# A fused adaLN, linear-attention and SwiGLU block: the order of the first query tiles, their PSUM banks and VectorE's list

## The chip, the cores and the metric

The kernel runs on one core of one Trainium2 chip. The metric is the device time of one execution in microseconds (us). Times of a kernel are medians over several executions; the profile is of one further execution. Below, PE is the matrix engine TensorE, PEld its weight loads, DVE is VectorE, ACT is ScalarE, POOL is GpSimd, and SP is the engine whose queue issues nearly all DMAs.

## The reference

One transformer block with x of 2048 rows and 1024 columns (bf16), a conditioning vector c, and a hidden width of 3584. Cut to what matters:

```python
sa, ca, ga, sb, cb, gb = split(silu(c) @ w_mod)          # six vectors of 1024
h = layernorm(x) * (1 + ca) + sa
q, k, v = heads(h @ wqkv)                                # 32 heads of 32
phi = lambda t: where(t > 0, t + 1, exp(t)) + 1e-6
pq, pk = phi(q), phi(k)
kv, z = einsum('bhsd,bhse->bhde', pk, v), einsum('bhsd->bhd', pk)
o = (pq @ kv) / (pq @ z + 1e-6)
x = x + ga * (o @ wo)
h = layernorm(x) * (1 + cb) + sb
x = x + gb * ((silu(h @ w_gate) * (h @ w_up)) @ w_down)
```

## The kernel before

The 2048 rows are 16 tiles of 128 rows, in four chunks of 512 rows. The columns of q and of k are eight tiles (`nt`) of 128 each, and the 1024 input columns are eight steps (`dt`) of a product. A q or k tile of one chunk is thus eight matmuls of 128 x 128 by 512 that accumulate in one PSUM bank. There are eight banks (0 to 7).

Instructions are recorded one after the other into a list for each engine (`_Prog`), and each engine runs its list strictly in order. Waits are derived from the recorded order: an instruction waits for the last conflicting access to its SBUF bytes, and for the last access of another engine to its PSUM bank. So the order in which the Python code records operations is the order of each engine's work, and an engine that waits holds back all that was recorded behind. All instructions appear in the profile with one line, that of the recorder (L176), so the tile names tell them apart.

The part that is changed runs in about the first 80 us. `HT[0]` and `HT[1]` hold the normalised, transposed and modulated input of the even and the odd chunks. Chunk 0 comes first, in `q_phase_chunk0`, while the weights are still being loaded: seven q tiles are kept open at the same time in the banks `qb = [1, 2, 3, 4, 6, 7, 5]`, and advance together step by step as weights and modulated input arrive (`q_part`). Bank 0 meanwhile takes the small products that give the modulation vectors (`mod_sc`: matmuls of one column) and the bias that stands in for the shift of `dt` 0 to 5 (`bias_mm`, read out by `bias_fin` into `BIASQ`). The second half of the `WSA` weights, which the last shift product needs, is among the late loads. `fin_sa` casts the product on DVE, and `bias_mm` needs its result. The eighth q tile is computed at the end, in bank 0, after `bias_fin` has emptied it. `h0_shift` then adds the shift to the four steps that did without it, for the k tiles.

`q_phi` evacuates each q tile on ACT (exp and relu with the bias), into four slots of `E1`/`RL` and four of `E1X`/`RLX`; `q_min` and `q_add` finish it on DVE. Between these, DVE prepares chunk 1: statistics of row tiles 5 to 7 (tile 4's are made on ACT by `act_stats`), reciprocal roots on POOL, `ln1_xn` (normalise), a transposing DMA on SP's queue for each row tile (`th_dma`), and `th_mod(1, ...)`, the modulation of `HT[1]`, in halves of 256 columns (row tiles 4 and 5, then 6 and 7).

After that come the k groups: `k_group(0, 0..7)` for chunk 0, then for each further chunk eight k groups and eight q groups. A group takes the next bank of `next_bank`. `phi_evac` evacuates it on ACT (exp into one of the four slots of `E1`, in turn) and DVE finishes two groups at a time (`phi_flush`). Between the groups, dictionaries (`kside` for chunk 0, `s1` to `s3` for chunks 1 to 3) hold side work by the number of the group it follows: statistics, normalisation, transposes and `th_mod` of the chunk after. `th_mod(2, dt)`, which prepares chunk 2's `HT[0]`, runs on ACT for odd `dt` and on DVE for even, after the q groups 9 to 11 of chunk 1. From there on the kernel goes through the linear attention and the feed-forward part, which the change does not touch.

The groups are counted by `next_bank` from 0 (chunk 0's first k group): 8 to 15 are chunk 1's k groups, 16 to 23 its q groups, 24 to 31 chunk 2's k groups.

Of the kernel before, what the change touches and what calls it, by code (L numbers as in the profile page):

```python
# [5 lines left out]
FP32 = mybir.dt.float32  # L6
# [3 lines left out]
ALU = mybir.AluOpType  # L10
# [252 lines left out]
def bass_adaLN_cond__linear_attn_block__swiglu_ffn__prompt_kernel(  # L263
# [22 lines left out]
    with ExitStack() as es:  # L286
# [6 lines left out]
        def T(name, off, shape, dt):  # L293
            n = 1
            for s_ in shape[1:]:
                n *= s_
            assert off % 32 == 0 and off + n * mybir.dt.size(dt) <= ARENA, (name, off, shape)
            return nc.alloc_sbuf_tensor_at(name, shape, dt, offset=base + off)
# [47 lines left out]
        RL = T("rl", 188 * KB, [128, 4, 512], BF16)  # L346
        E1X = T("e1x", 192 * KB, [128, 4, 512], BF16)
        RLX = T("rlx", 196 * KB, [128, 4, 512], BF16)
        ACC = T("acc", 192 * KB, [128, D], FP32)
        MHL = T("mhl", 196 * KB, [128, 2, D], BF16)  # L350
        MHLT = T("mhlt", 192 * KB, [128, 2 * NDT, 128], BF16)
# [131 lines left out]
        def ln1_xn(st, c0=0, c1=D):  # L483
            P.dve("tensor_scalar", out=XRES[:, st, c0:c1], in0=XRES[:, st, c0:c1],
                  scalar1=MV[:, st, 0:1], scalar2=RSTD[:, st:st + 1], op0=ALU.subtract, op1=ALU.mult)
# [7 lines left out]
        def th_dma(st):  # L493
            buf, j = (st // 4) % 2, st % 4
            xbar(HT[:, buf, :, j * 128:(j + 1) * 128], XRES[:, st, :])
# [12 lines left out]
        def mod_sc(w, c0, ms, kts=range(NDT)):  # L508
            for m in ms:
                for kt in kts:  # L510
                    P.pe("matmul", out=PS[:, 0, c0 + m:c0 + m + 1], lhsT=w[:, kt, m * 128:(m + 1) * 128],
                         rhs=SILUC[:, kt:kt + 1], start=mod_first[0], stop=(kt == NDT - 1), skip_group_check=True)
                    mod_first[0] = False
# [5 lines left out]
        def fin_sa(m, n, cast=False):  # L519
            if cast:  # L520
                P.dve("tensor_copy", out=MODTMP[:, m:m + n], in_=PS[:, 0, m:m + n])
            P.dve("tensor_copy", out=MODCOL[:, 1, m:m + n], in_=PS[:, 0, m:m + n])
# [5 lines left out]
        def h0_shift(dt):  # L528
            P.dve("tensor_scalar", out=HT[:, 0, dt, :], in0=HT[:, 0, dt, :], scalar1=MODCOL[:, 1, dt:dt + 1],
                  scalar2=None, op0=ALU.add)  # L530
# [47 lines left out]
        def act_stats(st, passes=(0, 1)):  # L578
            junk0 = HT[:, 1, 0:2, :] if st < 4 else JUNK1[:]
            for i in passes:  # L580
                fn_, sc_, acc_ = ((ACT.Identity, 1.0 / D, SUMX), (ACT.Square, D ** -0.5, SUMSQ))[i]
                P.act("activation", out=junk0, in_=XRES[:, st, :].rearrange("p (a b) -> p a b", a=2),
                      func=fn_, scale=sc_, accum_out=acc_[:, st:st + 1])
# [15 lines left out]
        def act_var(st):  # L599
            P.dve("scalar_tensor_tensor", out=MV[:, st, 1:2], in0=SUMX[:, st:st + 1], scalar=SUMX[:, st:st + 1],  # L600
                  in1=SUMSQ[:, st:st + 1], op0=ALU.mult, op1=ALU.subtract)
            P.dve("tensor_scalar", out=VE[:, st:st + 1], in0=MV[:, st, 1:2], scalar1=-1.0, scalar2=EPS, op0=ALU.mult,
                  op1=ALU.add)
# [8 lines left out]
        def ln1_xn_sum(st, c0=0, c1=D):  # L612
            P.dve("tensor_scalar", out=XRES[:, st, c0:c1], in0=XRES[:, st, c0:c1],
                  scalar1=SUMX[:, st:st + 1], scalar2=RSTD[:, st:st + 1], op0=ALU.subtract, op1=ALU.mult)

        def pool_pow(st):
            P.pool("tensor_tensor", out=RSTD[:, st:st + 1], in0=VE[:, st:st + 1], in1=NEGHALF[:, 0:1], op=ALU.pow)
# [78 lines left out]
        def q_part(nt, bank, dts):  # L696
            for dt in dts:
                P.pe("matmul", out=PS[:, bank, :], lhsT=WQK[:, dt, nt * 128:(nt + 1) * 128],
                     rhs=HT[:, 0, dt, :], start=(dt == 0), stop=(dt == 7))
# [3 lines left out]
        def next_bank():  # L703
            i = qk_ctr[0]
            qk_ctr[0] += 1
            return (1, 2, 3, 4, 6, 7, 5, 0)[i % 8] if i < 40 else i % 5 + 1

        def q_group(ch, nt):
            buf, bank = ch % 2, next_bank()
# [39 lines left out]
        def mod_row_b(bank, i, dst):  # L749
# [3 lines left out]
            P.wait_for("sp", [wr])  # L753
            P.dma("mdr%d" % i, dst[:], MDR[i].unsqueeze(0).to_broadcast([128, D]))

        def q_slot(nt):
            return (E1, RL) if nt < 4 else (E1X, RLX)

        def q_phi(nt, bank):
            for buf, fn_ in zip(q_slot(nt), (ACT.Exp, ACT.Relu)):  # L760
                P.act("activation", out=buf[:, nt % 4, :], in_=PS[:, bank, :], func=fn_, bias=BIASQ[:, nt:nt + 1])

        def q_min(nts):
            for nt in nts:
                e = q_slot(nt)[0][:, nt % 4, :]
                P.dve("tensor_scalar", out=e, in0=e, scalar1=1.0, scalar2=1e-6, op0=ALU.min, op1=ALU.add)

        def q_add(nts):
            for nt in nts:
                e, r = q_slot(nt)  # L770
                P.dve("tensor_tensor", out=PQT[:, nt, 0:512], in0=r[:, nt % 4, :], in1=e[:, nt % 4, :], op=ALU.add)

        def q_phase_chunk0():
            qb = [1, 2, 3, 4, 6, 7, 5]
            fin_ca(2, 2)
            for dt in (2, 3):
                h0_first(dt, "dve")
            for nts, dts in ((range(3), (0,)), (range(3), (1,)), ((3, 4, 5, 6), (0, 1))):
                for nt in nts:
                    q_part(nt, qb[nt], dts)  # L780
            for nt in range(7):
                if nt == 4:
                    mod_sc(WCA, 8, range(4, 8))
                    fin_ca(4, 4)
                    for dt in (4, 5):
                        h0_scale_only(dt)
                q_part(nt, qb[nt], (2, 3))
            act_stats(4, (0,))
            for nt in range(7):
                if nt == 6:  # L790
                    mod_sc(WSA, 0, range(6, 8))
                    fin_sa(6, 2)
                    for dt in (6, 7):
                        h0_scale(dt)
                q_part(nt, qb[nt], (4, 5))
            mod_sc(WSA, 0, range(4, 6))
            fin_sa(4, 2, True)
            for dt in (4, 5):
                h0_shift(dt)
            for nt in range(7):  # L800
                if nt == 2:
                    bias_mm((4, 5))
                q_part(nt, qb[nt], (6,))
            for nt in range(7):
                if nt == 1:
                    mod_sc(WSA, 0, range(4), range(4))
                if nt == 3:
                    mod_sc(WSA, 0, range(4), range(4, 8))
                    fin_sa(0, 4, True)
                    ln_ops[1][0]()  # L810
                if nt == 5:
                    bias_mm(range(4))
                    bias_fin()
                q_part(nt, qb[nt], (7,))
            ln_ops[1][1]()
            ln_ops[1][2]()
            ln1_rstd1(5)
            for i, dt in enumerate((4, 5, 0, 1, 2, 3, 6, 7)):
                P.pe("matmul", out=PS[:, 0, :], lhsT=WQK[:, dt, 896:1024], rhs=HT[:, 0, dt, :], start=(i == 0),
                     stop=(i == 7))  # L820
            for dt in range(4):
                h0_shift(dt)
            ln1_xn(5)
            th_dma(5)
            for nt in range(2):
                q_phi(nt, qb[nt])
            act_stats(4, (1,))
            for nt in range(2, 8):
                q_phi(nt, qb[nt] if nt < 7 else 0)
            for f in ln_ops[2]:  # L830
                f()
            act_var(4)
            pool_pow(4)
            for f in ln_ops[3]:
                f()
            ln1_rstd2(6)
            ln1_xn_sum(4)
            th_dma(4)
            q_min((0, 1))
            for st in (6, 7):  # L840
                ln1_xn(st)
                th_dma(st)
            q_add((0, 1))
            for nts in ((2, 3), (4, 5)):
                q_min(nts)
                q_add(nts)
            qk_ctr[0] = 0

        def add(d, k, f):
            d.setdefault(k, []).append(f)  # L850
# [1 line left out]
        kside = {}  # L852
        ln_ops = [ln1_stats_ops(4 + jj) for jj in range(4)]

        for c0 in (0, 256):
            for dt in range(NDT):
                add(kside, 1, lambda dt=dt, c0=c0: th_mod(1, dt, c0, c0 + 256))
        add(kside, 1, lambda: q_min((6, 7)))
        add(kside, 1, lambda: q_add((6, 7)))
        for jj, k in ((0, 3), (1, 4)):  # L860
            add(kside, k, lambda jj=jj: act_stats(10 + jj))
        q_phase_chunk0()
        for st in range(12, 16):
# [384 lines left out]
```

## Time and profile before

| | us |
|---|---|
| median of 3 executions | 828.32 |
| lowest and highest | 827.97, 828.67 |
| the profiled execution, device time | 827.71 |
| its span, first to last instruction | 826.0 |
| PE busy | 816.3 (99%) |
| DVE busy | 312.2 (38%) |
| ACT busy | 197.0 (24%) |
| POOL busy | 41.0 (5%) |

By stretches of the span (us busy of each engine, the granted PE clock is 1.00 in all):

| stretch | what runs | PE | DVE | ACT |
|---|---|---|---|---|
| 12.0 to 21.2 | q tiles of chunk 0, first steps | 9.12 of 9.20 | 2.33 | 2.02 |
| 21.2 to 29.3 | last steps, shift, bias, eighth q tile | 7.85 of 8.10 | 4.50 | 2.86 |
| 29.3 to 43.1 | k groups of chunk 0 | 13.69 of 13.80 | 13.10 | 13.77 |
| 43.1 to 56.9 | k groups of chunk 1 | 13.75 of 13.80 | 13.55 | 6.99 |
| 56.9 to 70.7 | q groups of chunk 1 | 13.75 of 13.80 | 11.98 | 10.97 |

How to read it: durations of neighbouring instructions overlap at their ends, so sums can come to a little more or less than the time passed. Matmul ends are modelled, and a few matmul records are missing; the distance from one matmul's start to the next is the more exact measure. A row of the timeline gives start, length, engine, line, operation, output and inputs, count, and in brackets how long the engine was idle before it and what released it.

### The profile page before, as it was taken

Reading aid. Unit: us, or ns where it says so; the run is one execution under the profiler, and the core shown is the slowest. Engines: PE = TensorE matmul, PEld = TensorE weight load, DVE = VectorE, ACT = ScalarE, POOL = GpSimd, SP = SyncE. Lnnn points to the kernel's source line nnn. Section 1 sums busy time; section 2 is a strip of 40 time slices with the busy share of each in tenths; the row PEclk is TensorE's granted clock in tenths of the full one; section 3 lists DMA queues with packets and bytes.
Section 4 is the critical chain, followed back from the end, with each engine's and each line's share of the span. In section 5 each row is a group of like instructions: output and inputs, shape, how many; then the busy total and the mean of one; then the engine's idle time right before and its main releaser. Section 6 shows DMA issues by size and latency. Waiting matters only on the chain.

```text
span 826.0 us, 10436 instructions
## 1 busy us (share of the span) xinstructions
PE 816.3 (99%) x4243; PEld 375.9 (46%) x4322; DVE 312.2 (38%) x672; ACT 197.0 (24%) x338; POOL 41.0 (5%) x58
## 2 busy tenths in 40 slices
PE   8999999999999999999999999999999999999998
PEld 4544444444444444444444444444444444444444
DVE  5798988477945521111221112122111111221111
ACT  4758642123341111011111101111110111111011
POOL 1110000000130000020000003000000300000000
DMA  9969756865698995600455570045557004553000
GB/s 316 297 139 223 167 159 149 181 175 211 149 253 245 296 249 153 166 26 26 136 151 151 153 174 25 23 131 153 151 152 182 27 19 126 151 152 88 0 26 26
DMA packets 199392, 119.32 MB, mean 144 GB/s; under 512 B 58024, under 2 KB 183088, under 8 KB 199344
## 3 DMA queue, kind: packets, MB, share of 16 engines
q1 hardware_dynamic: 199328, 118.65, 53.8%
q8 instruction: 34, 0.56, 0.3%
q14 instruction: 14, 0.11, 0.0%
q10 hardware_dynamic: 16, 0.00, 0.0%
HBM read 100.67 MB, written 4.33 MB: 127 GB/s over the span
## 4 chain that ended last, share of the span: by engine, by line
PE 98%; issue 1%; DMA 0%; DVE 0%; POOL 0%; SPq 0%
PE ps L176 98%; DMA xres<-in_A_x_dram 0%; POOL rstd L176 0%; DVE xres L176 0%; DVE stats L176 0%; SPq L176 0%; DVE ht L176 0%; DVE ve L176 0%; DVE mv L176 0%; DVE modcol L176 0%
## 5 line engine op out<-in xcount | busy, mean ns | idle before, releaser
L176 PE MATMUL ps<-h2t,gug 128*128 128x512 bf16 x878 | 210.1, 379 | 0.9
L176 PE MATMUL ps<-h2t,guu 128*128 128x512 bf16 x878 | 209.9, 379 | 0.9
L176 DVE TENSOR_TENSOR at<-sg,ps 128x512 bf16<-128x512 bf16 x112 | 77.0, 687 | 282.8 <-PE ps L176 270.6
L176 ACT ACTIVATE sg<-ps 128x512 bf16<-128x512 f32 x112 | 66.9, 597 | 309.7 <-PE ps L176 298.3
L176 PEld LDWEIGHTS ps<-h2t,guu 128*128 128x128 bf16 x896 | 87.7, 98 | 105.7
L176 PEld LDWEIGHTS ps<-h2t,gug 128*128 128x128 bf16 x896 | 87.6, 98 | 105.5
L176 PE MATMUL ps<-wd_a,at 128*128 128x512 bf16 (+1 forms) x502 | 111.9, 377 | 0.5
L176 PE MATMUL ps<-ht,wqk 128*128 128x512 bf16 x499 | 110.7, 379 | 0.9 <-DVE ht L176 0.2
L176 PE MATMUL ps<-wd_b,at 128*128 128x512 bf16 (+1 forms) x377 | 84.6, 377 | 0.4
L176 PEld LDWEIGHTS ps<-wd_a,at 128*128 128x128 bf16 x512 | 50.1, 98 | 59.6
L176 DVE TENSOR_TENSOR ut<-att,gb_b 128x512 bf16<-128x512 bf16 (+1 forms) x32 | 13.6, 426 | 167.5 <-ACT att L176 167.5
L176 PEld LDWEIGHTS ps<-ht,wqk 128*128 128x128 bf16 x512 | 49.2, 98 | 58.9 <-DVE ht L176 1.0
L176 ACT ACTIVATE att<-ps 128x512 bf16<-128x512 f32 (+1 forms) x32 | 17.4, 591 | 182.1 <-PE ps L176 182.1
L176 PEld LDWEIGHTS ps<-wd_b,at 128*128 128x128 bf16 x384 | 37.6, 98 | 44.7
L176 PE MATMUL ps<-pk,xres 128*128 128x512 bf16 x250 | 55.4, 379 | 0.6 <-issue 0.5
L176 PE MATMUL ps<-mw,pqt 128*128 128x512 bf16 x249 | 55.4, 379 | 0.5 <-issue 0.2
L176 POOL TENSOR_SCALAR h2t<-h2t,modcol 128x512 bf16<-128x512 bf16 x32 | 26.5, 846 | 383.0 <-DMA h2t<-xn 383.0
L176 ACT ACTIVATE e<-ps 128x512 bf16<-128x512 f32 x56 | 33.3, 611 | 31.8 <-PE ps L176 15.8
L176 ACT ACTIVATE junk<-xres 128x1024 bf16<-128x1024 bf16 x26 | 27.6, 1063 | 45.9 <-DVE xres L176 34.2
L176 PEld LDWEIGHTS ps<-mw,pqt 128*128 128x128 bf16 x256 | 24.8, 98 | 30.0 <-issue 0.5
L176 PEld LDWEIGHTS ps<-pk,xres 128*128 128x128 bf16 x256 | 24.6, 98 | 30.1 <-issue 1.3
L176 DVE SCALAR_TENSOR_TENSOR xres<-ps,xres 128x512 bf16<-128x512 f32 x32 | 21.5, 688 | 11.6 <-PE ps L176 11.3
(111 smaller groups left out, 337.8 us busy)
## 6 DMA issues: line engine op xcount, KB each, us to landing
gug<-in_B_w_gate_dram SPq DMA_DIRECT2D x56, 512.0 KB, 4.0
guu<-in_B_w_up_dram SPq DMA_DIRECT2D x56, 512.0 KB, 5.3
xres<-in_A_x_dram SPq DMA_DIRECT2D x20, 256.0 KB, 4.4
rb<-recip_den SPq DMA_DIRECT2D x8, 512.0 KB, 11.7
stgx<-in_w_mod_dram SPq DMA_DIRECT2D x2, 2048.0 KB, 9.3
wd_a<-in_B_w_down_dram SPq DMA_DIRECT2D x4, 1024.0 KB, 7.7
out_dram<-xres SPq DMA_DIRECT2D x31, 128.0 KB, 1.7
xres<-in_A_x_dram SPq DMA_DIRECT2D x3, 1024.0 KB, 6.5
```

Source lines behind the costliest of these rows:

```text
L176: return getattr(e, method)(**kw)
```

## The change

Four things are changed together. The dt=7 step of all seven open q tiles is done before the last shift products instead of between them, so tile 0 ends first; ACT copies it from its bank to a new SBUF tile `QRAW` (fp32), and the eighth q tile accumulates in tile 0's bank, its matmuls laid around the last shift products and the bias product. The q tiles are evacuated in the order `QORD` = 1 to 7, then 0 (from `QRAW`), and take their slots in that order. The bank rotation of `next_bank` starts with bank 0 and differs for the groups 24 to 39. DVE's list is put in another order: tile 4's variance and normalisation come earlier, its transpose goes out before tile 5's, the first half of `th_mod(1, ...)` moves from the side work into the end of `q_phase_chunk0`, the last four q tiles are finished after the fourth k group, and `act_stats(10)` and `act_stats(11)` on ACT follow one group later.

```diff
--- before.py
+++ after.py
@@ -346,6 +346,7 @@
         RL = T("rl", 188 * KB, [128, 4, 512], BF16)
         E1X = T("e1x", 192 * KB, [128, 4, 512], BF16)
         RLX = T("rlx", 196 * KB, [128, 4, 512], BF16)
+        QRAW = T("qraw", 202 * KB, [128, 512], FP32)
         ACC = T("acc", 192 * KB, [128, D], FP32)
         MHL = T("mhl", 196 * KB, [128, 2, D], BF16)
         MHLT = T("mhlt", 192 * KB, [128, 2 * NDT, 128], BF16)
@@ -703,7 +704,11 @@
         def next_bank():
             i = qk_ctr[0]
             qk_ctr[0] += 1
-            return (1, 2, 3, 4, 6, 7, 5, 0)[i % 8] if i < 40 else i % 5 + 1
+            if i < 24:
+                return (0, 2, 3, 4, 6, 7, 5, 1)[i % 8]
+            if i < 40:
+                return (0, 2, 3, 4, 6, 1, 7, 5, 0, 2, 3, 1, 4, 6, 7, 5)[i - 24]
+            return i % 5 + 1
 
         def q_group(ch, nt):
             buf, bank = ch % 2, next_bank()
@@ -753,22 +758,30 @@
             P.wait_for("sp", [wr])
             P.dma("mdr%d" % i, dst[:], MDR[i].unsqueeze(0).to_broadcast([128, D]))
 
+        QORD = (1, 2, 3, 4, 5, 6, 7, 0)
+
         def q_slot(nt):
-            return (E1, RL) if nt < 4 else (E1X, RLX)
-
-        def q_phi(nt, bank):
+            i = QORD.index(nt)
+            bufs = (E1, RL) if i < 4 else (E1X, RLX)
+            return [t[:, i % 4, :] for t in bufs]
+
+        def q_phi(nt, src):
             for buf, fn_ in zip(q_slot(nt), (ACT.Exp, ACT.Relu)):
-                P.act("activation", out=buf[:, nt % 4, :], in_=PS[:, bank, :], func=fn_, bias=BIASQ[:, nt:nt + 1])
+                P.act("activation", out=buf, in_=src, func=fn_, bias=BIASQ[:, nt:nt + 1])
 
         def q_min(nts):
             for nt in nts:
-                e = q_slot(nt)[0][:, nt % 4, :]
+                e = q_slot(nt)[0]
                 P.dve("tensor_scalar", out=e, in0=e, scalar1=1.0, scalar2=1e-6, op0=ALU.min, op1=ALU.add)
 
         def q_add(nts):
             for nt in nts:
                 e, r = q_slot(nt)
-                P.dve("tensor_tensor", out=PQT[:, nt, 0:512], in0=r[:, nt % 4, :], in1=e[:, nt % 4, :], op=ALU.add)
+                P.dve("tensor_tensor", out=PQT[:, nt, 0:512], in0=r, in1=e, op=ALU.add)
+
+        def q_pair(i):
+            q_min(QORD[i:i + 2])
+            q_add(QORD[i:i + 2])
 
         def q_phase_chunk0():
             qb = [1, 2, 3, 4, 6, 7, 5]
@@ -785,7 +798,6 @@
                     for dt in (4, 5):
                         h0_scale_only(dt)
                 q_part(nt, qb[nt], (2, 3))
-            act_stats(4, (0,))
             for nt in range(7):
                 if nt == 6:
                     mod_sc(WSA, 0, range(6, 8))
@@ -802,48 +814,48 @@
                     bias_mm((4, 5))
                 q_part(nt, qb[nt], (6,))
             for nt in range(7):
-                if nt == 1:
+                q_part(nt, qb[nt], (7,))
+                if nt == 0:
+                    P.act("activation", out=QRAW[:], in_=PS[:, qb[0], :], func=ACT.Copy)
+                    act_stats(4)
+            for i, dt in enumerate(range(NDT)):
+                if i == 1:
                     mod_sc(WSA, 0, range(4), range(4))
-                if nt == 3:
+                if i == 3:
                     mod_sc(WSA, 0, range(4), range(4, 8))
+                    ln_ops[1][0]()
                     fin_sa(0, 4, True)
-                    ln_ops[1][0]()
-                if nt == 5:
+                    ln_ops[1][1]()
+                    act_var(4)
+                    pool_pow(4)
+                if i == 5:
                     bias_mm(range(4))
                     bias_fin()
-                q_part(nt, qb[nt], (7,))
-            ln_ops[1][1]()
+                P.pe("matmul", out=PS[:, qb[0], :], lhsT=WQK[:, dt, 896:1024], rhs=HT[:, 0, dt, :], start=(i == 0),
+                     stop=(i == 7))
             ln_ops[1][2]()
             ln1_rstd1(5)
-            for i, dt in enumerate((4, 5, 0, 1, 2, 3, 6, 7)):
-                P.pe("matmul", out=PS[:, 0, :], lhsT=WQK[:, dt, 896:1024], rhs=HT[:, 0, dt, :], start=(i == 0),
-                     stop=(i == 7))
             for dt in range(4):
                 h0_shift(dt)
+            ln1_xn_sum(4)
+            th_dma(4)
             ln1_xn(5)
             th_dma(5)
-            for nt in range(2):
-                q_phi(nt, qb[nt])
-            act_stats(4, (1,))
-            for nt in range(2, 8):
-                q_phi(nt, qb[nt] if nt < 7 else 0)
+            for nt in QORD:
+                q_phi(nt, QRAW[:] if nt == 0 else PS[:, qb[nt % 7], :])
             for f in ln_ops[2]:
                 f()
-            act_var(4)
-            pool_pow(4)
             for f in ln_ops[3]:
                 f()
             ln1_rstd2(6)
-            ln1_xn_sum(4)
-            th_dma(4)
-            q_min((0, 1))
+            q_min(QORD[0:2])
             for st in (6, 7):
                 ln1_xn(st)
                 th_dma(st)
-            q_add((0, 1))
-            for nts in ((2, 3), (4, 5)):
-                q_min(nts)
-                q_add(nts)
+            q_add(QORD[0:2])
+            q_pair(2)
+            for dt in range(NDT):
+                th_mod(1, dt, 0, 256)
             qk_ctr[0] = 0
 
         def add(d, k, f):
@@ -852,12 +864,11 @@
         kside = {}
         ln_ops = [ln1_stats_ops(4 + jj) for jj in range(4)]
 
-        for c0 in (0, 256):
-            for dt in range(NDT):
-                add(kside, 1, lambda dt=dt, c0=c0: th_mod(1, dt, c0, c0 + 256))
-        add(kside, 1, lambda: q_min((6, 7)))
-        add(kside, 1, lambda: q_add((6, 7)))
-        for jj, k in ((0, 3), (1, 4)):
+        for dt in range(NDT):
+            add(kside, 1, lambda dt=dt: th_mod(1, dt, 256, 512))
+        for i in (4, 6):
+            add(kside, 3, lambda i=i: q_pair(i))
+        for jj, k in ((0, 4), (1, 5)):
             add(kside, k, lambda jj=jj: act_stats(10 + jj))
         q_phase_chunk0()
         for st in range(12, 16):
```

## The prediction

> **What bounds the kernel now.** I began with the page's chain of work that ended last, then asked which waits TensorE (PE) still has, then followed the engines that feed it through the first 77 us, where every edit lies.
>
> ```profile
> PE 98%; issue 1%; DMA 0%; DVE 0%; POOL 0%; SPq 0%
> ```
>
> Nearly the whole span is PE. The waits of PE and of its weight loads (PEld), asked from 20 us on:
>
> ```profile
> PE ps L176 <- issue: 0.6, 4, 0.2
> PE ps L176 <- DVE ht L176: 0.2, 1, 0.2
> ...
> PEld ps L176 <- DVE modcol L176: 1.0, 3, 0.4
> PEld ps L176 <- DVE ht L176: 1.0, 6, 0.2
> PEld ps L176 <- DVE pkt L176: 0.5, 1, 0.5
> PEld ps L176 <- DVE biasq L176: 0.3, 1, 0.3
> ```
>
> Each row is total us, times, longest. A waiting weight load mostly lies behind the running matmul, so what counts is the start-to-start distance of matmuls: 0.2158 us for 512 columns (10.79 us for 50), 0.025 us for one column. Beyond that I find in the part changed: 0.10 us before the dt=6 step (22.5), 0.06 at `bias_mm` (26.34), 0.05 at 44.7, when chunk 1's first group waits for `th_mod`, and 0.13 at 46.755, when its third group waits for a bank. That is all a perfect change could win: about 0.3 us of 828.
>
> So the question is what becomes late. VectorE (DVE) is the busiest feeder between 29 and 62 us, and ScalarE (ACT) waits for it; the timeline of ACT:
>
> ```profile
> 60.86 0.60 ACT L176 ACTIVATE e<-ps 128x512 bf16<-128x512 f32 x1 [0.42 <-DVE pkt L176]
> ...
> 69.62 0.59 ACT L176 ACTIVATE e<-ps 128x512 bf16<-128x512 f32 x1
> 70.09 0.60 ACT L176 ACTIVATE rl<-ps 128x512 bf16<-128x512 f32 x1
> 70.57 1.52 ACT L176 ACTIVATE ht<-ht,modcol 128x512 bf16<-128x512 bf16 x2
> ```
>
> The first row waits for DVE's evacuation (its E1 buffer), and from there ACT has no idle row until 77. The last row is `th_mod(2,5)` and `th_mod(2,7)`, ending at 71.40 and 72.09. Chunk 2's first group starts at 46.755 + 14 x 1.726 = 70.92 and needs dt=5 at 72.00 and dt=7 at 72.43. With the 0.06 from an end to PE's start (46.69 to 46.755), dt=7 has 0.27 us to spare. This is the smallest margin that I find.
>
> **The change part by part.** *PE, 23 to 31 us.* No matmul is added. From 23.32: five dt=6 matmuls, then all seven dt=7 ones 24.40 to 25.91, tile 7's dt=0 to 26.13, 16 columns of the shift product (0.40) to 26.53, dt=1,2 to 26.96, 16 more to 27.36, dt=3,4 to 27.79. DVE's cast and copy follow the product as at 26.05 to 26.28, so they end at 27.79, and `bias_mm` starts at 27.85: the same 0.06 wait. It takes 0.82 to 28.67, tile 7's last three end at 29.31. Before, tile 7 ended at 27.58 + 8 x 0.216 = 29.31. The first k group needs bank 0 free: `bias_fin` is at 28.84 to 29.01, 0.3 early. Before, tile 7 waited for no time on `bias_fin` either (spacing 0.215 at 27.58). Gain here: 0.
>
> *The copy.* Bank 1 is ready at 24.40 + 0.38; ACT has idled since 14 us. The nearest rows are a PSUM copy to bf16 (0.594) and an fp32 copy into SBUF with a scale (0.721), so it ends at 25.4 to 25.55; tile 7 needs the bank at 25.91. Cost 0, with 0.36 of cover; what it overran would be PE's. `act_stats(4)` behind it starts with its tile's landing at 25.52, as now, and its second pass fills 26.7 to 27.9, idle before.
>
> *ACT's q evacuation* starts with BIASQ: 29.1 instead of 27.59. The second stats pass (1.03 of the path) is no longer inside, so the eight pairs of 1.15 end at 38.25 instead of 37.77. Banks come free first for tile 1 (30.4; the k group there starts at 31.04), then with growing slack. `q_phi(0)` reads SBUF fp32: 0.721 against 0.70 to 0.79 from PSUM, nothing.
>
> *DVE's list,* spacings from the same operations before. `bias_fin` 28.84, aggregate, ve, four shifts 29.23, xn(4) 30.28, xn(5) 30.74, two statistics triples to 34.20; the POOL power needs 1.22 (33.42 to 34.64 before), so xn(6) runs at 35.42 with 0.65 idle; q_add 36.33, the pair 37.00, done at 38.08. Now comes the moved first half of `th_mod(1)`, 8 x 0.256, which waits for transposes 4 and 5; all that DVE does next, the evacuation of k groups 0 and 1 first, queues behind that wait, and ACT's k exps behind that.
>
> *SP's queue.* The four transposes before:
>
> ```profile
> 30.12 8.89 SPq L176 DMA_TRANSPOSE ht<-xres  x4
> 39.06 2.24 SPq L176 DMA_DIRECT2D xres<-in_A_x_dram  x4
> ```
>
> They were issued at 30.12, 34.07, 36.33 and 37.69 and landed at 37.4, 38.3, 41.0 and 41.8, after the last x load of the earlier burst (36.44) and each other. The change issues tile 4's at 30.9, tile 5's when SP is through with it (2.77 before, so about 33.7), the others at 36.0 and 37.4. I take 38.3 for the second landing, as before: the burst in front is the same. So `th_mod` starts at 38.4; if the landing holds nothing, 38.08; if tile 5 takes its predecessor's 4.2 and a further 0.9 behind it, 39.2. The x loads behind them go out at 38.8 instead of 39.06, nothing.
>
> On: first half to 40.45, evacuation 0,1 (1.62) to 42.07, second half to 44.12, evacuation 2,3 to 45.74, two q pairs of 1.08 to 47.90, and evacuation 4,5 starts, which was:
>
> ```profile
> 47.23 0.48 DVE L176 TENSOR_SCALAR e<-e 128x512 bf16<-128x512 bf16 x2
> ```
>
> DVE is **0.7 us late** here (0.35 if unheld, 1.5 at the far end). Why, though it holds the same work: it starts 1.5 us later, and two waits (0.65 for POOL, 0.3 for the landing) replace as much.
>
> *What it does to PE.* Gains: chunk 1's first group finds dt=k at 42.07 + 0.256(k+1) + 0.15, 0.3 or more ahead of 43.12 + 0.216k; its third group's bank is free at 45.2, needed at 46.57. So 0.18 is won. `act_stats(10)`, `(11)` move one group back on ACT and end at 47.1, before anybody needs ACT. The new rotation: each reuse from 24 on is 6 or more groups (10 us) after the last use, and 18's bank 3 is free at 59.19 + 0.7 against 60.38. From 47 to 61 DVE has nothing to catch up with, so ACT's 60.86 becomes 61.56, and `th_mod(2,5)` and `(2,7)` end 0.7 later. PE, now at 70.74, stalls 0.33 for dt=5 and 0.28 for dt=7, and goes on at 72.86 instead of 72.43.
>
> The sum: -0.18 + 0.61 = **+0.43 us** (0.7 - 0.27). From -0.18 (lateness under 0.09) over +0.1 (unheld) to +1.2 (far end). After 77 ACT idles again, and the lateness ends.
>
> The profiled execution took 827.71 us, 826.0 of them span; it becomes 828.14. The median is 0.61 above it, so 828.32 + 0.43 = **828.75 us**. A measurement of this kernel can tell about 0.2% (1.66 us) from no change.
>
> **The rivals.** (1) *The transposes land on their own time*, tile 5's before 38.1: 0.35 - 0.27 = +0.08, 828.4. For it: it is issued 0.4 earlier than the second one was. Against: all four landed in order of issue. The Trainium skill ("DMA: Bandwidth & Descriptors", Queues, rings and completion order) says that completion is not first-in-first-out per issuing engine; by that the landing need not wait for the burst. The rows here, all in order, neither show nor exclude it.
>
> (2) *The list is not late*: if POOL's wait or the evacuations come out 0.6 shorter, only the 0.18 is left, 828.1. That the interleaving fills nothing, because there was no gap to fill at tile 7, is part of all cases.
>
> (3) *Cover for late weights.* The second half of the shift weights landed at 24.86 and was used at 25.45; the use moves to 26.96. Where a timed run has them 1 us later than the profiled one, the change saves 0.5 to 1: 827.5. No row shows such a wait.
>
> (4) *Slower: DVE held at the transposes.* `th_mod` now stands ahead of the evacuations. It decides from a second landing at 39.6: the list is then 0.35 + 39.7 - 38.08 = 1.95 late, and PE waits at chunk 1's own `th_mod`, at group 18's bank and at chunk 2, the largest counting: 1.95 - 0.27 = 1.7. Tile 5 needing the first one's 7.3 us from 33.7 lands at 41.0 and gives 3.1; so 830.0 to 831.4. Against: that 7.3 was the wait for the burst ending at 36.4, over by then.
>
> (5) *Slower: the stall cools the clock.* At the start eight matmuls came 0.427 apart; eight such are 8 x 0.211 = 1.7 us: 830.4. Against: the granted clock is 1.00 in all stretches, and after the 0.13 wait the next spacing is 0.227. The Trainium skill ("TensorE: Matmul & The Clock Gate", A second HAM failure mode: psum-queue depth-cycling) warns that short idles while cycling through banks can make the clock oscillate. This kernel cycles through eight banks, and no row shows it.
>
> **How the numbers follow.** Forecast 0.50; (1) 0.20; (2) 0.12; (3) 0.07; (4) 0.08; (5) 0.03. Only (4) and (5) are past +1.66: slower 0.11. Faster by 1.66 needs more than all visible waits, 0.02 out of (3). Same 0.87. The range takes in all but (4), (5) and the tail of (3): from 828.1 less the 0.35 by which runs differ and part of (3), 827.5, to 828.32 + 1.2 + 0.35 = 829.9.
>
> **What would show it.** Right: no gap at 44.7 and 46.8; `th_mod` starting at about 38.4, at the second landing; evacuation 4,5 near 47.9; the first group of chunk 2 with weight loads waiting for ACT's ht, 0.6 us in all. Wrong: PE waiting for ACT's copy near 25.9, for tile 1's bank at 31, or not at all near 72; a matmul spacing of 0.427 after 12 us.

## The result, and the profile after

The changed kernel took **830.14 us** (median of 22 runs, 828.08 to 831.36); the kernel before, run beside it, 828.15 us (22 runs, 827.62 to 829.23). The ratio is 1.0021, with a 95% interval of [1.0015, 1.0027]: slower by about 0.2%, 1.7 us by the ratio. The runs of the changed kernel are not gathered round their median: 17 of 22 lie from 829.9 to 831.4, and five lie between 828.0 and 829.7. The profiled execution is of the larger group: 830.09 us, of them 828.3 span, against 827.71 and 826.0.

First the page's chain of work that ended last, then the waits of matmuls (PE) and of weight loads (PEld) from 30 to 80 us, all of the changed kernel:

```profile
PE 91%; DVE 3%; DMA 2%; SPq 2%; ACT 1%; issue 1%; POOL 0%; ACTq 0%; DVEq 0%
```

```profile
PE ps L176 <- DVE ht L176: 1.0, 1, 1.0
PE ps L176 <- ACT ht L176: 0.5, 1, 0.5
```

```profile
PEld ps L176 <- DVE ht L176: 2.7, 8, 1.5
PEld ps L176 <- ACT ht L176: 1.4, 2, 1.0
PEld ps L176 <- DVE pkt L176: 0.2, 1, 0.2
```

Before, PE held 98% of the chain. Now it leaves PE: 2% of it is a transfer and 2% SP's queue, where both had shown 0%. The two rows of PE were absent before: one wait for DVE's `ht`, one for ACT's. Their places, in the timeline of weight loads:

```profile
44.30 0.10 PEld L176 LDWEIGHTS ps<-ht,wqk 128*128 128x128 bf16 x1 [1.53 <-DVE ht L176]
44.56 0.10 PEld L176 LDWEIGHTS ps<-ht,wqk 128*128 128x128 bf16 x1 [0.16 <-DVE ht L176]
...
73.95 0.23 PEld L176 LDWEIGHTS ps<-ht,wqk 128*128 128x128 bf16 x2 [0.97 <-ACT ht L176]
74.65 1.41 PEld L176 LDWEIGHTS ps<-ht,wqk 128*128 128x128 bf16 x8 [0.47 <-ACT ht L176]
```

The first pair is chunk 1's first group, the second chunk 2's. From the start-to-start distances of the matmuls, less 0.216 each, PE lost 1.20 and then eight times 0.01 to 0.04, 1.50 in all, in the first, and 0.64 + 0.26 + 0.02 = 0.92 in the second. Less the 0.18 that the change wins (the gaps of before at 44.7 and 46.8 are gone) that is 2.24, and the span grew by 2.3. So nearly all the loss lies in these two groups. Both have one origin, which DVE's waits (28 to 80 us) and its timeline show:

```profile
DVE e L176 <- ACT e L176: 2.7, 4, 1.4
DVE ht L176 <- DMA ht<-xres: 2.4, 1, 2.4
DVE xres L176 <- POOL rstd L176: 0.4, 1, 0.4
```

```profile
37.11 0.76 DVE L176 TENSOR_TENSOR pqt<-rl,e 128x512 bf16<-128x512 bf16 x2
40.23 2.14 DVE L176 TENSOR_SCALAR ht<-ht,modcol 128x256 bf16<-128x256 bf16 x8 [2.36 <-DMA ht<-xres]
...
49.72 0.50 DVE L176 TENSOR_SCALAR e<-e 128x512 bf16<-128x512 bf16 x2
```

DVE was through with the q pair at 37.78 (forecast: 38.08) and stood for 2.4 us at the hoisted first half of `th_mod(1)` until tile 5's transpose landed at 40.13. The evacuations queued behind that wait: 0 and 1 reached PSUM at 42.68 (39.21 before), and 4 and 5, the marker of the prediction, began at 49.72 instead of 47.23, 2.49 late. ACT carried the lateness on without loss:

```profile
63.37 0.60 ACT L176 ACTIVATE e<-ps 128x512 bf16<-128x512 f32 x1 [0.42 <-DVE pkt L176]
...
73.07 1.52 ACT L176 ACTIVATE ht<-ht,modcol 128x512 bf16<-128x512 bf16 x2
```

60.86 had become 63.37 (+2.51), and `th_mod(2,5)` and `(2,7)` ended at 73.90 and 74.60 (71.40 and 72.10 before): +2.5. The source of it all stands in SP's timeline:

```profile
30.90 9.13 SPq L176 DMA_TRANSPOSE ht<-xres  x4
```

The transposes of tiles 4 and 5 were issued at 30.90 and 33.28, as forecast to half a microsecond, and landed at 37.70 and 40.13. Before, the first two had landed at 37.40 and 38.30.

**What came between them.** Beside the kernel's own queue (q1), queue q8 carries a 16 KB packet every now and then (the profile names its kind "instruction"). The transfers from 37.70 to 40.13 of the changed kernel, by queue (packets, MB, and their time as a share of 16 engines):

```profile
q1 hardware_dynamic: 1227, 0.31, 126.3%
q8 instruction: 1, 0.02, 2.6%
```

This packet began at 37.92. In the trace's records, 21 of the transposes' 256-byte packets that began 0.5 to 0.8 us later took 1.06 to 1.35 us each, where such a packet mostly takes about 0.02, and for about a microsecond hardly a new one began. Between the first and second landing of the kernel before (37.40 to 38.30) there is no q8 packet; its packet came at 38.62, behind the second landing, and it was the third transpose that landed late, at 41.00, where nothing waited closely. In each of the twelve profiles of this study the packet of this stretch is followed by such a group of 14 to 27 slow packets, which begins 0.1 to 1.0 us behind its start. (Such groups also occur at other times without a packet: before and after both have one near 34 us, while x loads land.)

### The profile page after: what moved, and what is told of

Same layout as the page of the kernel before. It is cut to its first block, busy times and chain, and to the rows that moved or that the text cites. A ratio compares the mean times of both kernels' runs of the same rounds, so it can differ in the third digit from the quotient of the medians.

```text
span 828.3 us, 10516 instructions
## 1 busy us (share of the span) xinstructions
PE 822.0 (99%) x4322; PEld 376.2 (45%) x4322; DVE 312.9 (38%) x672; ACT 197.6 (24%) x339; POOL 40.5 (5%) x58
## 4 chain that ended last, share of the span: by engine, by line
PE 91%; DVE 3%; DMA 2%; SPq 2%; ACT 1%; issue 1%; POOL 0%; ACTq 0%; DVEq 0%
PE ps L176 91%; SPq L176 2%; DMA xres<-in_A_x_dram 1%; DVE pkt L176 1%; DMA ht<-xres 1%; DVE ht L176 1%; ACT junk L176 1%; DVE stats L176 1%; DVE xres L176 0%; DVE e L176 0%; ACT ht L176 0%; ACT rl L176 0%; ACT e L176 0%; DVE pqt L176 0%; DVE mv L176 0%
## 5 line engine op out<-in xcount | busy, mean ns | idle before, releaser
L176 PE MATMUL ps<-ht,wqk 128*128 128x512 bf16 x512 | 112.7, 379 | 1.6 <-DVE ht L176 1.0
L176 PEld LDWEIGHTS ps<-wd_b,at 128*128 128x128 bf16 x384 | 37.6, 98 | 44.7
L176 ACT ACTIVATE e<-ps 128x512 bf16<-128x512 f32 x56 | 33.1, 609 | 33.7 <-PE ps L176 15.0
```

The lines of the kernel that those rows point to most:

```text
L176: return getattr(e, method)(**kw)
```

## The experiments

The theory: *landing*. The loss is the wait at the hoisted `th_mod` (the first half, moved ahead of the evacuation of k groups 0 and 1), and DVE waits there because tile 5's transpose sits behind the burst of x loads and behind the q8 packet. The main rival is that the new order of the lists is late by itself. A second question is whether it is the packet or the burst that makes the transpose late. Times are medians; each is compared with the kernel before on the same chip: 827.83 for the first four, 828.48 for the next four, 828.01 for the last two.

**The hoist undone**, the rest of the change kept:

```
-            for dt in range(NDT):
-                th_mod(1, dt, 0, 256)
...
-        for dt in range(NDT):
-            add(kside, 1, lambda dt=dt: th_mod(1, dt, 256, 512))
+        for c0 in (0, 256):
+            for dt in range(NDT):
+                add(kside, 1, lambda dt=dt, c0=c0: th_mod(1, dt, c0, c0 + 256))
```

> The changed kernel with the first half of th_mod(1) put back behind the evacuation of k groups 0 and 1. Theory H (VectorE is held at tile 5's transpose, which stands ahead of the evacuations): the wait of 2.36 us at 40.2 goes; the evacuation of groups 0 and 1 then waits for ScalarE's exps and starts near 39.5, the sixteen th_mod run from 40.8 to 44.9, evacuation of 4 and 5 starts near 48.7 instead of 49.72: PE loses 0.5 at chunk 1's first group and 1.2 in all against the kernel before (829.4). Rival I (the cost is the interleaving, which makes bias and q evacuation 1.5 us later): no change from the changed kernel, +1.7 to +2.0 against before.

829.33 us (11 runs); ratio 1.0014 [1.0005, 1.0023], or +1.2 by the ratio, as the theory expected. Tile 5's transpose landed late here too (40.16), but DVE did not wait for it. It waited for ACT's k exps instead; its timeline:

```profile
39.47 0.29 DVE L176 TENSOR_SCALAR e<-e 128x512 bf16<-128x512 bf16 x1 [1.16 <-ACT e L176]
...
41.39 4.19 DVE L176 TENSOR_SCALAR ht<-ht,modcol 128x256 bf16<-128x256 bf16 x16
...
49.26 0.50 DVE L176 TENSOR_SCALAR e<-e 128x512 bf16<-128x512 bf16 x2
```

Evacuation 4, 5 is 2.0 late even so, and PE lost 0.28 + 0.29 at chunk 1 and 0.65 + 0.26 at chunk 2. So the rest of the change costs over 1 us where nothing fills DVE's wait for ACT: the kernel before fills that time with a third q pair, which the change has moved behind the fourth k group. In the changed kernel the hoist fills it, and what it costs is its own wait.

**Tiles 4 and 5 transposed ahead of four x loads:**

```
-        for st in range(8, 12):
-            x_load(st)
...
             th_dma(5)
+            for st in (10, 11, 8, 9):
+                x_load(st)
```

> The changed kernel with the four loads of x tiles 8 to 11 issued behind tile 5's transpose instead of ahead of both transposes. Theory H: tiles 4 and 5 land by about 36.5, VectorE does not wait at th_mod, evacuation of groups 4 and 5 starts at 47.3 as in the kernel before, no PE wait at chunk 1 or chunk 2: 0.2 us faster than before (828.0). Rival I: the lateness stays, +1.5 to +2.0.

829.27 us (11 runs); ratio 1.0018 [1.0009, 1.0027], where -0.2 us was expected: a miss. Tiles 4 and 5 did land early (35.13 and 36.36), and the first half ran at once at 38.68. But the four x loads now lay ahead of tiles 6 and 7, which landed at 43.61 and 44.47, and the second half waited for them, in DVE's timeline:

```profile
38.68 2.14 DVE L176 TENSOR_SCALAR ht<-ht,modcol 128x256 bf16<-128x256 bf16 x8
...
44.56 2.14 DVE L176 TENSOR_SCALAR ht<-ht,modcol 128x256 bf16<-128x256 bf16 x8 [2.12 <-DMA ht<-xres]
```

The wait moved by one half and cost the same.

**The packet moved by PE's instructions.** Warm-up matmuls replaced so that PE has 44 instructions more:

```
-        warm(13, bank=3)
+        warm(10, bank=3)
+        for _ in range(25):
+            P.pe("matmul", out=PS[:, 3, 0:1], lhsT=IDENT[:], rhs=E1[:, 0, 0:1], start=True, stop=True)
```

> The changed kernel with three of the 13 warm-up matmuls replaced by 25 matmuls of one column, so that PE has 44 more instructions at the start and the 16 KB packet of the instruction queue (at 37.92 us, followed by a stand-still of the transposes' packets from 38.7 to 39.6) comes about 4.7 us earlier. Theory F (the packet is PE's instruction fetch, and it stops transposes that are in flight): tile 5 lands near 38.9 instead of 40.1, VectorE is 1.25 us late, about +1.0 against before. Rival L (the landing is set by the loads in front of it): lands at 40.1 as now, +1.7 to +2.0.

831.01 us (5 runs, 829.56 to 831.30); ratio 1.0034 [1.0022, 1.0047]. A miss: the packet came at 37.20 and not far ahead, once more 0.2 behind tile 4's landing (36.99), and tile 5 landed at 39.41. DVE waited 1.3 us for it. The next packet did come 4 us earlier (63.41 against 67.45). The profiled execution is the fastest of the five; why the others are 1.1 to 1.7 us slower than it stays open.

**The hoist alone**, on the kernel before:

```
+            for dt in range(NDT):
+                th_mod(1, dt, 0, 256)
             qk_ctr[0] = 0
...
-        for c0 in (0, 256):
-            for dt in range(NDT):
-                add(kside, 1, lambda dt=dt, c0=c0: th_mod(1, dt, c0, c0 + 256))
+        for dt in range(NDT):
+            add(kside, 1, lambda dt=dt: th_mod(1, dt, 256, 512))
```

> The kernel before with one part of the change alone: the first half of th_mod(1) moved ahead of the evacuation of k groups 0 and 1. Theory H (what costs is the landing, not the place): tiles 4 and 5 land at 38.3, when VectorE gets there (38.4); evacuation of 4 and 5 starts 0.4 us earlier than before, both PE waits (44.7, 46.8) go: -0.2 us. Rival P (the place alone costs): VectorE waits there as in the changed kernel, +1.5 or more.

828.07 us (11 runs, 827.59 to 829.52); ratio 1.0006 [0.9997, 1.0015]. Inconclusive: no difference can be told. In its profile the packet (38.85) came 0.19 behind the second landing (38.66), DVE began `th_mod` at 38.76, and PE had no gap from 30 to 80 us; but some runs are 1 to 2 us longer.

**The PE side alone**, with the lists of DVE, ACT and SP in the order of before:

```
-            ln1_xn_sum(4)
-            th_dma(4)
             ln1_xn(5)
             th_dma(5)
...
             ln1_rstd2(6)
+            ln1_xn_sum(4)
+            th_dma(4)
...
-            for dt in range(NDT):
-                th_mod(1, dt, 0, 256)
+            q_pair(4)
...
-        for jj, k in ((0, 4), (1, 5)):
+        for jj, k in ((0, 3), (1, 4)):
```

> The changed kernel with VectorE's list, SP's queue and the two act_stats in the order of the kernel before: what is left of the change is the early dt=7 step, the copy to QRAW, the eighth tile in tile 0's bank, the evacuation order and the bank rotation. Theory I' (bias_fin 1.5 us later makes VectorE's list late, of which its waits for POOL, ScalarE and x tiles give back about 0.6): evacuation of groups 0 and 1 ends 0.9 later (41.3), the sixteen th_mod end at 45.4, PE loses 0.9 at chunk 1's first group: +0.6 to +0.9 against before. Rival N (the interleaving is free, all the cost is in the rebuilt list): 0 to -0.1.

828.85 us (11 runs); ratio 1.0007 [0.9999, 1.0016]: +0.37, between the two expectations and within what can't be told. Its profile is of an execution with late transfers (829.8 us, the second half of the shift weights landing at 26.36 instead of 24.86), so it doesn't split the cost further.

**All x loads behind the four transposes**, on the changed kernel:

```
-        for st in range(8, 12):
-            x_load(st)
...
         q_phase_chunk0()
-        for st in range(12, 16):
+        for st in (10, 11, 8, 9, 12, 13, 14, 15):
             x_load(st)
```

> The changed kernel with the loads of x tiles 8 to 11 behind all four transposes. In the run with them behind tile 5's alone, VectorE's wait went from the first half of th_mod(1) to the second. Theory H: tiles 4 and 5 land before 37, tiles 6 and 7 before 42, no wait of VectorE for a transpose, no PE wait at chunk 1 or 2: 0.2 us faster than the kernel before. Rival I (the later bias is the cost, as it was in the list's start): +0.6 or more stays.

828.22 us (11 runs); ratio 0.9995 [0.9987, 1.0004]. The landings were 34.66, 35.90, 40.77 and 41.60, the packet came at 38.35. DVE's waits from 28 to 60 us hold no row for a transfer, and PEld's from 30 to 80 are down to one of 0.3, with no gap of PE:

```profile
DVE modtmp L176 <- PE ps L176: 1.1, 1, 1.1
DVE xres L176 <- POOL rstd L176: 0.4, 1, 0.4
```

```profile
PEld ps L176 <- ACT ht L176: 0.3, 1, 0.3
```

The packet now falls ahead of tile 6's landing, and the second half of `th_mod` (41.91) found tile 7's only 0.3 us old. With the two early transposes ahead of both the x loads and the packet, the whole loss is gone, and the rest of the change is kept. The main rival, a list that is late by itself, would have kept +0.6 or more.

**The packet later**, by 16 PE instructions fewer on the changed kernel (`warm(13, ...)` to `warm(9, ...)` and `warm(5, ...)` to `warm(1, ...)`):

> The changed kernel with eight warm-up matmuls fewer at the start (13 to 9, 5 to 1), so that PE's instruction list is 16 instructions shorter up to any later point and the 16 KB packet that came at 37.92 us should come about 1.7 us later. Theory F (the packet stops the transposes that follow it): it comes after tile 5's transpose, which lands 0.9 after tile 4's, at 38.6 instead of 40.1; VectorE is 1.0 late instead of 2.5: +0.6 to +0.8 against before. Rival L (the landing has another cause): 40.1 as now, +1.7 to +2.0.

828.64 us (11 runs, only 828.35 to 828.91); ratio 1.0002 [0.9993, 1.0011]. The packet came 1.8 us later than in the changed kernel (39.74), behind both landings, which now lay 0.89 apart (37.81, 38.70); tile 6's was the late one, 2.93 behind. DVE's timeline:

```profile
38.79 2.14 DVE L176 TENSOR_SCALAR ht<-ht,modcol 128x256 bf16<-128x256 bf16 x8 [0.54 <-DMA ht<-xres]
```

PE lost nothing at chunk 1, 0.49 + 0.26 at chunk 2. The burst and SP's order were untouched here, so this separates the packet from the burst: without the packet between the two landings the second came 1.43 earlier (38.70 against 40.13). The wait shrank by 1.82, of which 0.4 is something else: PE and DVE ran 0.4 us later in this execution (`bias_mm` at 28.23 instead of 27.83). That the packet came late in all eleven executions is inferred from their times; the profile shows one. The time came out lower than the 0.6 to 0.8 expected, by half a microsecond that is not explained.

**The hoist with two x loads only ahead**, on the kernel before (the hoist's own edit as above):

```
-        for st in range(8, 12):
+        for st in range(10, 12):
             x_load(st)
...
-        for st in range(12, 16):
+        for st in (8, 9, 12, 13, 14, 15):
             x_load(st)
```

> The kernel before with the first half of th_mod(1) ahead of the evacuation of groups 0 and 1, as in the run with that part alone, and the loads of x tiles 8 and 9 behind the four transposes. Theory H: the landing of tiles 4 and 5 comes about 1.3 us earlier and is no longer on the edge; both PE waits of the kernel before go, and the slow executions of the hoist alone (828.8, 829.5) too: -0.2 us against before. Rival: the hoist keeps costing what it cost alone, +0.2.

828.21 us (11 runs); ratio 0.9999 [0.9990, 1.0008]: not to be told from before; the medians differ by 0.27 the expected way. The slow executions did not all go: one of the eleven took 830.03.

**The changed kernel and the all-behind version side by side:**

> The changed kernel itself, beside the next one on the same chip: +1.7 to +2.0 us against before, as in its own measurement, most executions with tile 5's transpose landing past 39.5 and a few, below 829, with it landing in time.

> The changed kernel with the loads of x tiles 8 to 11 behind all four transposes, once more, on the same chip as the changed kernel. If the loads in front of the transposes and the packet behind tile 4's are the whole cost, it is 1.9 to 2.2 us faster than the changed kernel and 0.2 to 0.3 faster than the kernel before; if its first result was the chip's, it lies at the kernel before or above.

The changed kernel took 829.52 us (11 runs, 827.73 to 830.70); ratio 1.0021 [1.0012, 1.0030]. With all x loads behind: 827.88 us (11 runs, 827.40 to 828.42); ratio 0.9999 [0.9990, 1.0008]. The second is 1.64 us below the first, where 1.9 to 2.2 was expected, and not to be told from the kernel before.

The profiled execution of the changed kernel was this time its fastest, 827.73 us. It shows the same program without the wait; DVE's timeline, and PEld's waits from 30 to 80 us:

```profile
37.41 0.76 DVE L176 TENSOR_TENSOR pqt<-rl,e 128x512 bf16<-128x512 bf16 x2
38.09 2.14 DVE L176 TENSOR_SCALAR ht<-ht,modcol 128x256 bf16<-128x256 bf16 x8
...
47.59 0.49 DVE L176 TENSOR_SCALAR e<-e 128x512 bf16<-128x512 bf16 x2
```

```profile
PEld ps L176 <- ACT ht L176: 0.3, 1, 0.3
```

Tiles 4 and 5 landed at 36.94 and 37.84, the packet came at 38.27. `th_mod` follows the q pair at once, evacuation 4, 5 begins 0.36 later than before, and PE has no gap in this stretch. Against the first profile the landing is 2.29 earlier and the execution 2.36 shorter.

**A race of two events.** In the eight profiles of the table the two transposes stand behind all four x loads: the first one lands 0.95 to 0.97 us after the last of these, and the second would land 0.9 later. The rows go by whether the packet begins before that point:

| profile | burst ends | second landing due (+1.86) | packet | second landing |
|---|---|---|---|---|
| before | 36.44 | 38.30 | 38.62 | 38.30 |
| hoist alone | 36.80 | 38.66 | 38.85 | 38.66 |
| changed, second profile | 35.98 | 37.84 | 38.27 | 37.84 |
| packet later | 36.85 | 38.71 | 39.74 | 38.70 |
| changed, first profile | 36.75 | 38.61 | 37.92 | 40.13 |
| hoist undone | 36.94 | 38.80 | 38.13 | 40.16 |
| packet shifted (44 more) | 36.03 | 37.89 | 37.20 | 39.41 |
| PE side alone | 37.48 | 39.34 | 38.90 | 41.01 |

Where the packet is last, the second landing is on time in all four; where it is first, it is 1.4 to 1.7 late in all four. The margin of the kernel before is 0.3 us, and it has no hoisted `th_mod` that would wait.

## Why the prediction was right and wrong

**The number.** Forecast was +0.43 us; measured was +1.7 by the ratio, where 1.66 was named as what can just be told. 830.14 is just outside the range's upper end of 829.9, and so is the ratio applied to the median that the prediction started from, 828.32 x 1.0021 = 830.06. The mechanism that most executions seem to follow is rival (4), given 0.08: the profiled one does, and the times of 17 of 22 lie with it.

**The step that failed** is the landing, under *SP's queue*: "I take 38.3 for the second landing, as before: the burst in front is the same." The burst was the same (its last load landed at 36.75 instead of 36.44); the landing was 40.13, 1.8 later, with the packet (37.92) between the two landings. The trace of before held it: its own third landing came 2.7 behind the second, with the 16 KB packet at 38.62 between them. Read as a hazard that can fall between any two landings, it gives a second landing of 38.3 + 1.4 to 1.7, just past the 39.6 from which rival (4) was said to decide. Instead the prediction set the 7.3 us of the first transpose against that rival ("that 7.3 was the wait for the burst ending at 36.4, over by then"). That was true, but it did not exclude another cause of lateness.

The far end of the range rested on this step too, and does not come out of its own terms: 33.7 + 4.2 + 0.9 is 38.8, not 39.2. With 0.1 to the start of `th_mod` it gives +0.9 instead of +1.2 and an upper end of 829.6.

**Rival (4)** was sized rightly: 1.7 of cost for a lateness of 1.95 (its terms add up to 1.97), "830.0 to 831.4", against most runs in 829.9 to 831.4. Its rule, lateness less 0.27, gives 2.49 - 0.27 = 2.22 for the profiled execution; 2.24 was counted in PE's gaps. One part was off: chunk 1 and chunk 2 do not overlap so that "the largest" counts. PE lost 1.50 at chunk 1, and at chunk 2 only what was left, 0.92; the total is set by the lateness all the same, because a stall at chunk 1 delays PE's need at chunk 2 by as much.

**Rival (1)**, tile 5's transpose landing before DVE needs it, is what the changed kernel's second profile shows (37.84 against 38.09), though not by passing the burst: the transposes landed in order of issue behind it. The Trainium skill ("DMA: Bandwidth & Descriptors", Queues, rings and completion order) says that completion is not first-in-first-out per issuing engine. In all profiles here the transposes landed in the order of their issue, and behind the x loads issued ahead of them, so no run here shows it.

**Right, by the rows:** the copy by ACT ran from 24.80 to 25.40 (25.4 to 25.55 forecast) and PE didn't wait for it; tile 7 won nothing, the 0.06 at `bias_mm` stayed; `q_phi` began at 29.08 (29.1) and ended at 38.29 (38.25), although the form that reads SBUF took 0.82 and not 0.721 (these records overlap; from start to start it was 0.61, against 0.57 from PSUM); xn(4) and xn(5) at 30.27 and 30.73 (30.28, 30.74). The waits at 44.7 and 46.8 are gone where nothing is held. `th_mod(2,5)` and `(2,7)` were the place with the smallest margin, and pass the lateness on one to one.

**Sized wrongly:** the lateness without a wait at the landing. The wait for POOL's power was 0.40 instead of 0.65, so xn(6) and the q pair came 0.3 early, and the list itself is about 0.05 late, not 0.35. The second profile bears this out: evacuation 4, 5 begins 0.36 later than before, but PE runs 0.32 later in that execution (`bias_mm` at 28.15 against 27.83), so the list is 0.04 late against PE. The two profiles with all x loads behind give the same (47.74 and 47.68, with `bias_mm` at 28.30 and 28.25). That is under the 0.09 from which a cost was expected: PE shows no gap, and the execution took 827.73, 0.02 from before's profile, where the prediction had +0.1 for this case. So what the change does when nothing waits at the landing is rival (2), the list not being late.

**Rival (5)**, the clock: after the 1.20 us stall the granted clock is 1.00. The next seven distances are 0.254 to 0.259, the pace of `th_mod`, for which these matmuls wait (8 x 0.256); those behind them are 0.216 to 0.227. The page's row for the whole span:

```profile
PEclk9999999999999999999999999999999999999999
```

The Trainium skill ("TensorE: Matmul & The Clock Gate", A second HAM failure mode: psum-queue depth-cycling) warns of short idles while cycling through banks. With eight banks and a stall of 1.2 us the clock did not fall here: all 33 runs of the changed kernel have a mean granted clock of 1.00.

**What stays open:** what sets the moment of the packet. The packet after it follows PE's instruction count: 70.11 with 16 fewer and 63.41 with 44 more, against 66.27 to 67.96 in the ten profiles where the count is unchanged. For the packet of this stretch this can't be told. With the count unchanged it came anywhere from 37.92 to 40.42 (the latest with tiles 4 and 5 ahead of the x loads), and 39.74 with 16 fewer lies inside that. In seven of the eight rows of the table it began 0.2 to 0.5 us behind a landing, so that the time of its request and of its start can't be told apart here. That the packet causes the slow group behind it rests on the race and on the one experiment that moved it past both landings; it is likely, and not shown. What is shown is that the late landing is the loss: where no landing is late, by another order of the loads or by chance, the loss is gone.

## What to carry to other kernels

When a wait is hoisted ahead of work that others need, price it by the worst landing that any transfer of that kind shows in the profile, not by the landing that the same slot had: here a landing at 40.13 made DVE wait 2.4 us with the hoist, and one at 40.16 made nothing wait without it. Where several transfers share a queue, issue the ones that something waits for ahead of the bulk loads; here all x loads had to go behind all four transposes, and with only the first two ahead the wait moved to the other two. A profile is one execution: if the margin between two events is 0.3 us, both orders will be met.

## What the runs showed of the hardware

A 128 x 1024 bf16 transpose from SBUF to SBUF lands 0.9 us behind its predecessor in the queue when nothing intervenes (37.40 to 38.30), and 2.3 to 2.6 behind it when a 16 KB packet of the instruction queue comes between the two (37.70 to 40.13). In that time the packet itself took only 0.99 us, but 256-byte packets in flight took up to 1.35 us instead of about 0.02. The next packets of this kind began at 67.45, 95.15 and 123.57, 28 to 30 us apart.
